# Causal mask as additions on GpSimd, and a new order of row blocks, in a fused attention, MoE and GLU kernel

## The chip, the cores and the metric

The kernel runs on one core of one Trainium2 chip. The metric is the time of one execution on the device, in microseconds (us); it is given as the median of several runs. One more execution of the same program is recorded by the profiler, and all rows below are from that one.

## What is computed

Three stages follow one another, all in fp32: causal attention with a bias made of cumulated sums (4 batches x 8 heads, 576 rows, 64 columns a head), a mixture of 8 experts in which each token goes to its best one (2304 tokens, 512 columns, 1024 hidden), and a gated unit (1536 hidden) behind an RMS norm. The change touches the attention stage.

```python
def _attn_ref(q, k, v, s):
    scores = scale * np.matmul(q, k.transpose(0, 1, 3, 2))
    causal = np.triu(np.ones((S, S), dtype=bool), k=1)
    cum = np.cumsum(np.maximum(s, 0.0), axis=-1)
    bias = -(cum[:, :, :, None] - cum[:, :, None, :])
    scores = np.where(causal, -1000000000.0, scores + np.minimum(bias, 0.0))
    attn = np.exp(scores - np.max(scores, axis=-1, keepdims=True))
    attn = attn / (np.sum(attn, axis=-1, keepdims=True) + 1e-09)
    return np.matmul(attn, v)
...
    x = _moe_ref(x=x, **moe_kwargs)      # argmax of x @ w_gate picks the expert
    return _moe2_ref(x=x, **moe2_kwargs) # (silu(xn @ w_gate) * (xn @ w_val)) @ w_out
```

## The kernel before

**Tiles.** Attention goes over 16 pairs of heads, numbered 0 to 15. The two heads of a pair lie on partitions 0 to 63 and 64 to 127, so their matmuls have 64 rows each. The 576 rows of a head make four row blocks of 128 (i = 0 to 3) and 64 last rows, those of both heads in one block (i = 4). Row block i needs the columns 0 to 128 (i + 1).

**One pair, by the names in the code.**
- `s_mm(p, i)`: for a row block two matmuls of scores (L272, one for each head, in two passes of fp32), four small bf16 matmuls that add the causal mask to the last 128 columns (L275, from the tiles `pick` and `mask`), and for each head one VectorE reduction (`reduced`, L258) that adds the cumulated sums `st.cb`, writes the scores to a tile `sc` and their extreme to `nm`. For the 64 last rows: two matmuls from `st.bd` (L285), which holds the last q columns of both heads on its diagonal blocks; GpSimd copies them there (`q_diag`, L245, two copies per pair).
- `s_exp`: ScalarE's exponential with its sum (L298), one per head and row block.
- `t_mm(p, g)`: seven groups of transposes on TensorE (L317, g = 0 to 6), each followed by ScalarE's copy into `pt` (L350).
- `pv_mm` (L363, L367): the products with v; `pv_out` (L373, L375): ScalarE's copies of the result into `vp`; `o_mm` (L391): matmuls that bring the result back into token rows and give the gate's logits; VectorE scales them (L395, L398).
- `attn_load`, `load_bias`, `load_v`: the loads of the pair after next, on the SP queue, into three input buffers (p % 3).

**What sets the order.** `attention` makes a plan: each piece of pair p has a position 10 p + POS[tag], and the pieces are issued sorted by position. With POS, the scores of pair p stand beside the transposes of pair p - 1, and the PV products of pair p - 1 follow. TensorE, VectorE, ScalarE and SP run in just that order. GpSimd's order is made by the framework's scheduler, which may put an instruction ahead of earlier ones.

**Other work in the plan.** After every four pairs (a batch), `route` ranks the tokens of the batch by expert on VectorE and then scatters their rows to `xs` in memory by five indirect DMAs on GpSimd (L485). Eight pieces of the first expert's weights are split into a high and a low part at the positions PIECES: a cast on ScalarE (L670) and a subtraction on GpSimd (L671), after which SP asks for the next raw piece. At EARLY_AT the first expert's first tokens are loaded, gated (ScalarE, L742) and transposed.

**Banks.** All PSUM tiles of attention come from one ring of eight banks, tag "b"; a tile's first matmul waits until the reader of the tile eight allocations earlier is done. The tiles `sc` form a ring of four.

Of the kernel before, what the change touches and what calls it, by code (L numbers as in the profile page):

```python
# [90 lines left out]
def masks(k):  # L91
# [3 lines left out]
    mk = slot(k, 8, [128], name="mk")  # L95
    nc.gpsimd.memset(mk, 0.0)
# [39 lines left out]
def cumulate(k):  # L136
    nc = k.nc
# [9 lines left out]
    for h in range(2):  # L147
        ps = k.psum.tile([128, 512], F32, name=f"cb{h}", tag="b")
        nc.tensor.matmul(ps[:, 0:256], k.ident[0:32, h:h + 1].broadcast_to((32, 128)), d[:, 0:256], start=True, stop=True)
        nc.scalar.copy(k.st[0].cb[:, h, 0:256], ps[:, 0:256])  # L150
# [31 lines left out]
SPLIT = ((0, 576), (576, 1152), (1152, 2176), (2176, 2752), (2752, 2880))  # L182


def attn_statics(k):
# [5 lines left out]
    def inputs(q, kk, cb, cm, bd):  # L191
        nc.gpsimd.memset(bd[0:64, 64:128], 0.0)
        nc.gpsimd.memset(bd[64:128, 0:64], 0.0)
        k.inp.append((q, kk, cb.rearrange("p (h n) -> p h n", h=2), cm, bd))
# [3 lines left out]
    inputs(first[:, 2880:3456], first[:, 3456:4032], second[:, 2880:3904], pp[0][:, 3200:3776], pp[1][:, 3200:3328])  # L198
# [27 lines left out]

def load_bias(k, p):
    st = k.st[p]
    c = 256 if p == 0 else 0
    for h in range(2):  # L230
        k.nc.sync.dma_start(out=st.cb[:, h, c:512], in_=k.cumd[2 * p + h:2 * p + h + 1, c:512].broadcast_to((128, 512 - c)))
# [11 lines left out]
def q_diag(k, p, h):  # L243
    st, r = k.st[p], slice(64 * h, 64 * h + 64)
    k.nc.gpsimd.tensor_copy(st.bd[r, r], st.q[r, 512:576])  # L245
# [16 lines left out]
def s_mm(k, p, i):  # L262
# [4 lines left out]
    if i < 4:  # L267
# [3 lines left out]
        for h, r in enumerate(rows):  # L271
            nc.tensor.matmul(ps[h], st.q[r, 128 * i:128 * i + 128], st.k[r, 0:w], start=True, stop=False)  # L272
        for n in range(2):
# [3 lines left out]
        for h in range(2):  # L277
            sc = st.s[i, h] = A.tile([128, S], F32, name=f"sc{p}_{i}_{h}", tag="sc", bufs=4)
            reduced(k, sc[:, 0:w], ps[h], st.cb[:, h, 0:w], st.nm[:, 2 * i + h:2 * i + h + 1])
# [135 lines left out]
def route(k, b):  # L415
# [66 lines left out]
    for t in range(5):  # L482
# [6 lines left out]
        of_rows(k, "placed", i.ins, k.filled)  # L489
# [142 lines left out]

# [29 lines left out]
def split(k, n=1, refill=True):  # L662
    nc = k.nc
    for _ in range(n):
        if k.staged:
# [5 lines left out]
            nc.gpsimd.tensor_tensor(w[:, :, 1, :], raw, w[:, :, 0, :].bitcast(F32), op=ALU.subtract)  # L671
# [1068 lines left out]
```

## Time and profile before

| | us |
|---|---|
| median of 3 runs | 867.74 |
| lowest and highest of them | 867.0, 867.84 |
| the profiled execution | 866.87 |
| its span, first to last instruction | 865.1 |

The profile's page gives busy time by engine: TensorE (PE) 840.1 us, VectorE (DVE) 507.6, ScalarE (ACT) 454.4, GpSimd (POOL) 365.9. Attention fills about the first 190 us. In rows of a timeline, the first number is the start in us from the span's start, the second how long the instructions of the row took together; engine, line of the kernel, operation, out<-in and shapes follow; "x4" means four instructions in a row, and a bracket tells how long the engine was idle before them and what ended that. A busy TensorE isn't one at its peak: matmul ends are modelled.

### The profile page before, as it was taken

Reading aid. Unit: us, or ns where it says so; the run is one execution under the profiler, and the core shown is the slowest. Engines: PE = TensorE matmul, PEld = TensorE weight load, DVE = VectorE, ACT = ScalarE, POOL = GpSimd, SP = SyncE. Lnnn points to the kernel's source line nnn. Section 1 sums busy time; section 2 is a strip of 40 time slices with the busy share of each in tenths; the row PEclk is TensorE's granted clock in tenths of the full one; section 3 lists DMA queues with packets and bytes.
Section 4 is the critical chain, followed back from the end, with each engine's and each line's share of the span. In section 5 each row is a group of like instructions: output and inputs, shape, how many; then the busy total and the mean of one; then the engine's idle time right before and its main releaser. Section 6 shows DMA issues by size and latency. Waiting matters only on the chain.

```text
span 865.1 us, 15488 instructions
## 1 busy us (share of the span) xinstructions
PE 840.1 (97%) x5522; PEld 750.3 (87%) x5522; DVE 507.6 (59%) x1241; ACT 454.4 (53%) x1069; POOL 365.9 (42%) x318
## 2 busy tenths in 40 slices
PE   6999999989999999999999999999999999999994
PEld 4777777779899999999999999999999988888883
DVE  5557575745415435545799988888888778400000
ACT  4988988882866565655543443333333244432310
POOL 3000431052686667677221334444444350466641
PEclk9999999999999999999999999999999999999997
DMA  6999786034575556556662332432332486521001
GB/s 208 295 325 298 251 247 201 30 118 144 197 237 191 176 175 214 185 187 194 225 191 74 128 107 104 146 112 86 103 105 102 142 325 277 204 89 38 36 37 41
DMA packets 60506, 141.45 MB, mean 164 GB/s; under 512 B 6992, under 2 KB 25451, under 8 KB 60419
## 3 DMA queue, kind: packets, MB, share of 16 engines
q1 hardware_dynamic: 57459, 130.83, 46.3%
q0 software_dynamic: 2912, 9.46, 2.9%
q8 instruction: 45, 0.74, 0.4%
q14 instruction: 42, 0.34, 0.1%
q10 hardware_dynamic: 48, 0.07, 0.0%
HBM read 105.42 MB, written 34.92 MB: 162 GB/s over the span
## 4 chain that ended last, share of the span: by engine, by line
PE 47%; DVE 3%; DMA 1%; ACT 1%; issue 1%; POOL 0%; POOLq 0%; DVEq 0%; ACTq 0%
PE gg L1166 28%; PE go L1482 17%; PE g L807 1%; DMA ringa<-ytd 1%; DVE raw L1095 0%; DVE ws L1143 0%; DVE gx1a L1410 0%; DVE raw L1098 0%; DVE h L791 0%; DVE ringa L1062 0%; DVE raw L1125 0%; DVE raw L1094 0%; DVE sq L832 0%; DVE tmp L1188 0%; DVE tmp L1186 0%
## 5 line engine op out<-in xcount | busy, mean ns | idle before, releaser
L671 POOL TENSOR_TENSOR u<-raw,u 128x1024 fp32r<-128x1024 f32 x64 | 154.8, 2429 | 73.5 <-ACT u L670 73.3
L807 PE MATMUL g<-h,u 128*128 128x256 f32 (+7 forms) x768 | 105.9, 295 | 0.7 <-DVE h L791 0.4
L787 PE MATMUL g<-xt,u 128*128 128x256 f32 (+7 forms) x768 | 104.2, 295 | 0.0
L807 PEld LDWEIGHTS g<-h,u 128*128 128x128 f32 x768 | 101.4, 188 | 1.8 <-DVE h L791 0.9
L787 PEld LDWEIGHTS g<-xt,u 128*128 128x128 f32 x768 | 101.4, 188 | 0.8
L1204 POOL TENSOR_TENSOR hs<-tmp,hs 128x384 f32<-128x384 f32 x27 | 30.3, 1123 | 106.5 <-ACT hs L1202 106.5
L258 DVE CUSTOM_DVE_ANT_0 sc<-s,in 128x128 f32<-128x128 f32 (+3 forms) x128 | 57.8, 489 | 29.2 <-ACT vp L375 16.1
L298 ACT ACTIVATE p<-sc,nm 128x128 f32<-128x128 f32 (+3 forms) x128 | 71.0, 573 | 6.8 <-DVE nm L258 6.8
L670 ACT CAST u<-raw 128x1024 fp32r<-128x1024 f32 x64 | 67.3, 1051 | 2.7 <-DMA raw<-in_w 2.7
L1166 PE MATMUL gg<-gx2a,ws 128*128 128x384 f32 x360 | 67.4, 335 | 0.6 <-DVE tmp L1188 0.6
L1166 PE MATMUL gg<-gx0a,ws 128*128 128x384 f32 x360 | 67.7, 336 | 0.0
L1166 PE MATMUL gg<-gx1a,ws 128*128 128x384 f32 x360 | 67.1, 335 | 0.0
L1487 DVE COPY raw<-go 128x256 f32<-128x256 f32 x1 | 0.4, 425 | 108.1 <-ACT raw L1486 108.1
L1166 PEld LDWEIGHTS gg<-gx2a,ws 128*128 128x128 f32 x360 | 62.8, 188 | 0.9 <-DVE tmp L1188 0.9
L1166 PEld LDWEIGHTS gg<-gx0a,ws 128*128 128x128 f32 x360 | 63.1, 188 | 0.0
L1166 PEld LDWEIGHTS gg<-gx1a,ws 128*128 128x128 f32 x360 | 62.7, 188 | 0.0
L350 ACT COPY pt<-t 128x512 f32<-128x512 f32 (+3 forms) x160 | 56.2, 449 | 10.0 <-PE t L317 8.9
L815 DVE TENSOR_TENSOR sq<-sq,sn 128x256 f32<-128x256 f32 (+6 forms) x21 | 12.7, 607 | 81.7 <-ACT sn L814 81.7
L317 PE MATMUL t<-ident,p 128*128 128x128 f32 x400 | 51.8, 275 | 0.0
L1096 ACT ACTIVATE raw<-raw 128x512 f32<-128x512 f32 x36 | 24.6, 683 | 51.7 <-DVE raw L1095 34.1
L363 PE MATMUL pvy<-pt,vp 128*64 128x512 f32 (+4 forms) x320 | 46.8, 427 | 2.9 <-ACT pt L350 2.9
L272 PE MATMUL s<-in 64*128 64x128 f32 (+3 forms) x256 | 49.5, 495 | 0.0
(307 smaller groups left out, 1704.5 us busy)
## 6 DMA issues: line engine op xcount, KB each, us to landing
raw<-in_w SPq DMA_DIRECT2D x64, 512.0 KB, 3.9
hd<-hs SPq DMA_DIRECT2D x72, 192.0 KB, 1.9
in<-cumd SPq DMA_DIRECT2D x30, 256.0 KB, 7.8
xs<-zrow SPq DMA_DIRECT2D x8, 771.0 KB, 7.1
raw<-in_wg SPq DMA_DIRECT2D x12, 512.0 KB
raw<-in_wv SPq DMA_DIRECT2D x12, 512.0 KB, 4.8
raw<-in_wo SPq DMA_DIRECT2D x12, 512.0 KB, 8.0
vp<-in_v SPq DMA_DIRECT2D x16, 320.0 KB
```

The source lines that it names most:

```text
L258: k.nc.vector.tensor_tensor_reduce(out=out, in0=ps, in1=bias, scale=-0.125, scalar=3e38, op0=ALU.add, op1=ALU.min, accum_out=accum)
L272: nc.tensor.matmul(ps[h], st.q[r, 128 * i:128 * i + 128], st.k[r, 0:w], start=True, stop=False)
L298: k.nc.scalar.activation(out, st.s[i, h][:, 0:w], AF.Exp, bias=st.nm[:, n:n + 1], scale=-1.0, accum_out=acc)
L317: nc.tensor.transpose(ps[:, off:off + 128], src[:, 128 * j:128 * j + 128], k.ident)
L350: nc.scalar.copy(b, a)
L363: nc.tensor.matmul(st.y[r, a - 64:512], st.v[:, h, j, :], k.pt[:, h, o:o + S - a], start=j == 0, stop=j == 4)
L670: nc.scalar.copy(w[:, :, 0, :], raw)
L671: nc.gpsimd.tensor_tensor(w[:, :, 1, :], raw, w[:, :, 0, :].bitcast(F32), op=ALU.subtract)
L787: nc.tensor.matmul(ps[:, 0:n], w[:, f % 4, a, 128 * kc:128 * kc + 128], x[b][:, kc, 0:n], start=kc == 0 and i == 0, stop=kc == 3 and i == 2)
L807: nc.tensor.matmul(ps[:, 0:n], w[:, f % 4, a, 128 * c:128 * c + 128], k.h[b][:, f, 0:n], start=f == 0 and i == 0, stop=f == 7 and i == 2)
L1166: k.nc.tensor.matmul(k.ps[u, bank], w[:, a, 128 * c:128 * c + 128], x[:, b, GT * c:GT * c + GT], start=first and c == 0 and n == 0, stop=c ...
L1482: k.nc.tensor.matmul(acc[g][t], c[:, a, cols], w[:, b, :], start=f == 0 and i == 0, stop=f == NF - 1 and i == 2)
```

## The change

- Pairs 1 to 15 get no mask matmuls; pair 0 keeps them. Instead GpSimd adds the mask to the cumulated sums of a head: `sums` now has six blocks of 128 per head; the four with the sums are blocks 2 to 5, and two more hold masked copies. `mask_sums(p, 0)` (one addition 128x512, one 128x256, for the first two row blocks and the last one) stands a little behind pair p - 1's first scores; `mask_sums(p, 1 + h)` (128x256 each, one per head), for row block 2, stands behind row block 1's reduction, since it writes over blocks that this reduction reads. VectorE reads the masked blocks by `bias_of`.
- The row blocks go in the order 0, 1, 3, 2, and so do their exponentials.
- `in_turn` makes GpSimd's copies of q_diag, its indirect DMAs and its weight subtractions follow the latest second `mask_sums` ahead of them in the plan.
- New positions: ROUTE, PIECES (casts now between the copies of the transposes of pairs 8 and 9), EARLY_AT (the gate behind the last pair's copies). One input buffer gets a tile of its own for the sums.

```diff
--- before.py
+++ after.py
@@ -92,8 +92,9 @@
     nc, P = k.nc, k.apool
     k.identb = P.tile([128, 128], BF16, name="identb")
     nc.vector.tensor_copy(k.identb, k.ident)
-    mk = slot(k, 8, [128], name="mk")
-    nc.gpsimd.memset(mk, 0.0)
+    k.mz = P.tile([128, 2, 128], F32, name="mz")
+    nc.gpsimd.memset(k.mz, 0.0)
+    mk = k.mz[:, 0, :]
     nc.gpsimd.affine_select(out=mk, in_=mk, compare_op=ALU.is_ge, fill=NEG, base=0,
                             pattern=[[-1, 128]], channel_multiplier=1)
     k.pick = P.tile([128, 2, 128], BF16, name="pick")
...
@@ -191,11 +192,12 @@
     def inputs(q, kk, cb, cm, bd):
         nc.gpsimd.memset(bd[0:64, 64:128], 0.0)
         nc.gpsimd.memset(bd[64:128, 0:64], 0.0)
-        k.inp.append((q, kk, cb.rearrange("p (h n) -> p h n", h=2), cm, bd))
+        k.inp.append((q, kk, cb.rearrange("p (h b n) -> p h b n", h=2, b=6), cm, bd))
 
     inputs(*(first[:, a:b] for a, b in SPLIT))
     attn_load(k, 0)
-    inputs(first[:, 2880:3456], first[:, 3456:4032], second[:, 2880:3904], pp[0][:, 3200:3776], pp[1][:, 3200:3328])
+    inputs(first[:, 3392:3968], second[:, 3392:3968], A.tile([128, 1536], F32, name="cb2"), pp[0][:, 3200:3776],
+           pp[1][:, 3200:3328])
     inputs(*(second[:, a:b] for a, b in SPLIT))
     w = slot(k, 3, [3200], name="vp")
     k.vv = [w[:, 640 * n:640 * n + 640].rearrange("p (h j d) -> p h j d", h=2, j=5) for n in range(3)]
@@ -224,11 +226,37 @@
     nc.sync.dma_start(out=st.k, in_=k.k[p])
 
 
+def sums(st, h):
+    return st.cb[:, h, 2:6, :].rearrange("p b n -> p (b n)")
+
+
+def mask_sums(k, p, n):
+    G, cb = k.nc.gpsimd, k.st[p].cb
+    sh = (128, 2, 2, 128)
+    if n == 0:
+        m = k.mz[:, 0, :].unsqueeze(1)
+        in_turn(k, G.tensor_tensor(cb[:, :, 0:2, :], cb[:, :, 3:1:-1, :], m.unsqueeze(1).broadcast_to(sh), op=ALU.add))
+        in_turn(k, G.tensor_tensor(cb[:, :, 5, :], cb[:, :, 5, :], m.broadcast_to((128, 2, 128)), op=ALU.add))
+    else:
+        h = n - 1
+        k.turn = [G.tensor_tensor(cb[:, h, 0:2, :], cb[:, h, 4:2:-1, :], k.mz, op=ALU.add).ins]
+
+
+def in_turn(k, i):
+    after(k, i.ins, k.turn)
+    return i
+
+
+def bias_of(st, i, h):
+    c = st.cb[:, h]
+    return (c[:, 1:2, :], c[:, 2::-2, :], c[:, 2::-1, :], c[:, 2:6, :])[i]
+
+
 def load_bias(k, p):
     st = k.st[p]
     c = 256 if p == 0 else 0
     for h in range(2):
-        k.nc.sync.dma_start(out=st.cb[:, h, c:512], in_=k.cumd[2 * p + h:2 * p + h + 1, c:512].broadcast_to((128, 512 - c)))
+        k.nc.sync.dma_start(out=sums(st, h)[:, c:512], in_=k.cumd[2 * p + h:2 * p + h + 1, c:512].broadcast_to((128, 512 - c)))
     for h in range(2):
         k.nc.sync.dma_start(out=st.cm[64 * h:64 * h + 64, :], in_=k.cumd[2 * p + h:2 * p + h + 1, :].broadcast_to((64, S)))
 
@@ -242,7 +270,7 @@
 
 def q_diag(k, p, h):
     st, r = k.st[p], slice(64 * h, 64 * h + 64)
-    k.nc.gpsimd.tensor_copy(st.bd[r, r], st.q[r, 512:576])
+    in_turn(k, k.nc.gpsimd.tensor_copy(st.bd[r, r], st.q[r, 512:576]))
 
 
 def copy(k, eng, out, in_):
@@ -269,14 +297,20 @@
         rows = (slice(0, 64), slice(64, 128))
         ps = [k.psum.tile([128, 512], F32, name=f"s{p}_{i}_{h}", tag="b")[:, 0:w] for h in range(2)]
         for h, r in enumerate(rows):
-            nc.tensor.matmul(ps[h], st.q[r, 128 * i:128 * i + 128], st.k[r, 0:w], start=True, stop=False)
-        for n in range(2):
+            nc.tensor.matmul(ps[h], st.q[r, 128 * i:128 * i + 128], st.k[r, 0:w], start=True, stop=p > 0)
+        for n in range(2 if p == 0 else 0):
             for h, r in enumerate(rows):
                 nc.tensor.matmul(ps[h][:, w - 128 + 64 * n:w], k.pick[r, n, :], k.mask[r, n, 64 * n:128],
                                  start=False, stop=n == 1)
         for h in range(2):
             sc = st.s[i, h] = A.tile([128, S], F32, name=f"sc{p}_{i}_{h}", tag="sc", bufs=4)
-            reduced(k, sc[:, 0:w], ps[h], st.cb[:, h, 0:w], st.nm[:, 2 * i + h:2 * i + h + 1])
+            acc = st.nm[:, 2 * i + h:2 * i + h + 1]
+            if p == 0:
+                reduced(k, sc[:, 0:w], ps[h], sums(st, h)[:, 0:w], acc)
+            else:
+                reduced(k, *(t.rearrange("p (b n) -> p b n", n=128) for t in (sc[:, 0:w], ps[h])), bias_of(st, i, h), acc)
+                if i == 1:
+                    mask_sums(k, p, 1 + h)
     else:
         sc = st.s[4, 0] = A.tile([128, S], F32, name=f"scm{p}", tag="sc", bufs=4)
         for n in range(2):
@@ -486,7 +520,7 @@
             out=k.xs, out_offset=bass.IndirectOffsetOnAxis(ap=ix[0:n, t:t + 1], axis=0),
             in_=xt[0:n, t, :], in_offset=None,
         )
-        of_rows(k, "placed", i.ins, k.filled)
+        of_rows(k, "placed", in_turn(k, i).ins, k.filled)
         k.placed.append(i.ins)
     if b == B - 2:
         V.tensor_scalar(k.na, k.base[0:1, 0:1], float(NA), None, op0=ALU.min)
@@ -566,15 +600,17 @@
     Q=[-4.0, -3.9],
     Z=[-18.4, -18.3, -7.8],
 )
-ROUTE = (34.1, 0.2)
+TURN = dict(S=(0, 1, 3, 2, 4), X=(0, 1, 2, 3, 6, 7, 4, 5, 8))
+MASK = -9.7
+ROUTE = (35.2, 0.22)
 FR = 2
-PIECES = (80.0, 81.5, 90.0, 91.5, 159.0, 161.7, 164.4, 167.1)
-EARLY_AT = (152.2, 164.0, 170.2, 170.3)
+PIECES = (81.8, 84.0, 91.8, 94.0, 159.0, 161.7, 165.3, 167.1)
+EARLY_AT = (152.2, 165.25, 170.2, 170.3)
 FILL = (12.6, 12.7, 12.8, 22.6, 22.7, 22.8, 32.5, 32.6)
 
 
 def attention(k):
-    k.st, k.todo = {}, []
+    k.st, k.todo, k.turn = {}, [], []
     with ExitStack() as es:
         k.apool = es.enter_context(k.tc.tile_pool(name="attn", bufs=1))
         cum = cumulate(k)
@@ -601,7 +637,7 @@
 
         for p in range(NP):
             for tag, fn in (("S", s_mm), ("X", s_exp), ("T", t_mm), ("V", pv_mm), ("W", pv_out), ("O", o_mm)):
-                for i, at in enumerate(POS[tag]):
+                for i, at in zip(TURN.get(tag, range(9)), POS[tag]):
                     add(10 * p + at, fn, k, p, i)
             add(10 * p + POS["N"][0], s_norm, k, p)
             for h, at in enumerate(POS["Q"]):
@@ -609,6 +645,8 @@
             for fn, at in zip((attn_load, load_bias, load_v), POS["Z"]):
                 if p > 1:
                     add(10 * p + at, fn, k, p)
+            if p:
+                add(max(10 * p + MASK, 0.6), mask_sums, k, p, 0)
             j = route(k, p // 4)
             if p == NP - 1:
                 k.last = j
...
@@ -668,7 +706,7 @@
                 new_unit(k, s, u)
             w = k.wt[s, u][:, q:q + 2]
             nc.scalar.copy(w[:, :, 0, :], raw)
-            nc.gpsimd.tensor_tensor(w[:, :, 1, :], raw, w[:, :, 0, :].bitcast(F32), op=ALU.subtract)
+            in_turn(k, nc.gpsimd.tensor_tensor(w[:, :, 1, :], raw, w[:, :, 0, :].bitcast(F32), op=ALU.subtract))
             if refill:
                 feed(k)
 
```

GpSimd's queue about pair 8, before. `in14` is the input buffer of pair 8, `in03` that of pair 9, `p16` and its copies belong to pair 10, and `xs` is where the tokens are scattered. The copies of pairs 8 and 9 are ahead of the five DMAs, and the copy that waits for the DMAs' queues (DMASW) is one for pair 10.

```order
L245 COPY in14_144<-in14_144 64x64 [waits DMAHW7_49,PE_49,Pool_49]
L245 COPY in03_143<-in03_143 64x64 [waits DMAHW6_49,PE_49,Pool_49]
L485 DMA xs_60<-xt0_539,ix0_1143 21504x514 [waits DMAHW3_49,DMAHW2_49,DMAHW4_49,DMAHW1_49,DMAHW5_49,DVE_49,Pool_49]
L485 DMA xs_60<-xt0_539,ix0_1143 21504x514 x4
L245 COPY p16_146<-in03_143 64x64 [waits DMAHW7_49,PE_49]
L245 COPY p16_146<-in03_143 64x64 [waits DMASW3_49,DMASW2_49,DMASW4_49,DMASW1_49,DMASW0_49]
L671 TENSOR_TENSOR u13_1381<-raw10_1028,u13_1381 128x2x512 [waits DMAHW5_49,Activation_49,Pool_49]
```

The same place after. `cb2` holds the sums of pair 7, `in13` is the input buffer of pair 8 with its sums, `mz` the mask. L238 and L239 are `mask_sums(8, 0)`, L273 the copies of q_diag, L242 `mask_sums(p, 1)` and `(p, 2)`.

```order
L242 TENSOR_TENSOR cb2_151<-cb2_151,mz_126 128x256 [waits DVE_49,Pool_49]
L242 TENSOR_TENSOR cb2_151<-cb2_151,mz_126 128x256 [waits DVE_49]
L238 TENSOR_TENSOR in13_144<-in13_144,mz_126 128x2x256 [waits DMAHW2_49,DMAHW1_49,Pool_49]
L239 TENSOR_TENSOR in13_144<-in13_144,mz_126 128x2x128
L519 DMA xs_60<-xt0_518,ix0_1089 21504x514 [waits DMAHW5_49,DMAHW4_49,DMAHW3_49]
L519 DMA xs_60<-xt0_518,ix0_1089 21504x514 x4
L273 COPY in13_144<-in13_144 64x64 [waits DMAHW7_49,PE_49]
L273 COPY in13_144<-in13_144 64x64 [waits DMASW2_49,DMASW3_49,DMASW1_49,DMASW4_49,DMASW0_49,Pool_49]
L242 TENSOR_TENSOR in13_144<-in13_144,mz_126 128x256 [waits DVE_49,Pool_49]
L242 TENSOR_TENSOR in13_144<-in13_144,mz_126 128x256 [waits DVE_49]
```

The copies of pair 8 are now behind the DMAs, and pair 8's two additions of row block 2 behind those copies. About pair 12 the queue is the same, with batch 1's DMAs.

ScalarE's queue at the last pair, before; `t15_g` are the transposes of pair 15, L742 is the gate, L670 the casts of weight pieces.

```order
L350 COPY pt8_160<-t15_4_2725 128x2x256
L742 ACTIVATE x0_2608<-x0_2608 128x512 x2
L670 CAST u23_2736<-raw21_2686 128x2x512
L350 COPY pt8_160<-t15_5_2739 128x2x128
L350 COPY pt8_160<-t15_5_2739 128x2x2x64
L350 COPY pt8_160<-t15_6_2746 128x2x64 x3
L670 CAST u23_2736<-raw22_2705 128x2x512
L373 COPY vp7_155<-pvx15_2760 128x64
```

The same place after:

```order
L384 COPY pt7_161<-t15_4_2546 128x2x256
L384 COPY pt7_161<-t15_5_2555 128x2x128
L384 COPY pt7_161<-t15_5_2555 128x2x2x64
L384 COPY pt7_161<-t15_6_2562 128x2x64 x3
L780 ACTIVATE x0_2429<-x0_2429 128x512 x2
L708 CAST u22_2571<-raw20_2507 128x2x512
L708 CAST u22_2571<-raw21_2526 128x2x512
L407 COPY vp6_156<-pvx15_2581 128x64
```

The gate and one cast moved from ahead of the copies of transposes 5 and 6 to behind them, and both casts now stand between the gate and the copies of the PV result.

## Rows read from the trace of the kernel before

**Rows 1.** Table by stretches: from:to, length, busy us of each engine, clock, DMA.
```profile
20.00:40.00 20.00, 20.00 (x179) 14.15 (x178) 11.82 (x57) 19.14 (x65) 0.93 (x4) 1.00 1.06 302
...
80.00:100.00 20.00, 20.00 (x181) 15.05 (x178) 12.31 (x60) 18.26 (x57) 6.43 (x10) 1.00 0.95 298
...
180.00:200.00 20.00, 17.07 (x157) 15.12 (x154) 10.60 (x42) 12.92 (x31) 10.27 (x5) 1.00 0.26 80
```

**Rows 2.** Timeline of TensorE, from pair 5's scores to pair 6's.
```profile
59.15 0.49 PE L272 MATMUL s<-in 64*128 64x128 f32 x4
59.48 0.25 PE L275 MATMUL s<-mask,pick 64*128 64x128 bf16 x4
59.56 0.68 PE L272 MATMUL s<-in 64*128 64x256 f32 x4
...
60.98 1.11 PE L272 MATMUL s<-in 64*128 64x512 f32 x4
61.92 0.25 PE L275 MATMUL s<-mask,pick 64*128 64x128 bf16 x4
62.10 1.42 PE L317 MATMUL t<-ident,p 128*128 128x128 f32 x11
...
64.61 0.93 PE L317 MATMUL t<-ident,p 128*128 128x128 f32 x7
...
67.29 1.08 PE L363 MATMUL pvy<-pt,vp 128*64 128x512 f32 x4
...
70.15 0.49 PE L272 MATMUL s<-in 64*128 64x128 f32 x4
```

**Rows 3.** Timeline of TensorE, the last pair's PV.
```profile
187.89 1.08 PE L363 MATMUL pvy<-pt,vp 128*64 128x512 f32 x4 [2.94 <-ACT pt L350]
```

**Rows 4.** Timeline of TensorE, the second pass of row block 3 in pair 5.
```profile
61.49 0.60 PE L272 MATMUL s<-in 64*128 64x512 f32 x2
```

**Rows 5.** Groups by line on GpSimd: additions of a later stage.
```profile
L1143 POOL TENSOR_TENSOR ws<-raw,ws 128x512 fp32r<-128x512 f32 x20 | 29.4, 1484 | 18.5 <-ACT ws L1138 18.5
...
L1143 POOL TENSOR_TENSOR ws<-raw,ws 128x256 fp32r<-128x256 f32 x5 | 4.1, 837 | 3.0 <-ACT ws L1138 3.0
```

**Rows 6.** Timeline of VectorE, pair 5's reductions of row blocks 1 to 3.
```profile
60.47 0.42 DVE L258 CUSTOM_DVE_ANT_0 sc<-s,in 128x256 f32<-128x256 f32 x1
...
61.28 0.56 DVE L258 CUSTOM_DVE_ANT_0 sc<-s,in 128x384 f32<-128x384 f32 x1
...
62.32 0.69 DVE L258 CUSTOM_DVE_ANT_0 sc<-s,in 128x512 f32<-128x512 f32 x1
```

**Rows 7.** Timeline of GpSimd, the scatters of batches 0 and 1.
```profile
85.95 1.15 POOL L485 DMA_INDIRECT xs<-xt,ix  x1 [0.63 <-POOL in L245]
...
91.20 0.91 POOL L485 DMA_INDIRECT xs<-xt,ix  x1 [0.30 <-issue]
...
99.12 0.23 POOL L245 COPY p<-in 64x64 f32<-64x64 f32 x1 [3.09 <-DMA xs<-xt,ix]
...
131.72 0.90 POOL L485 DMA_INDIRECT xs<-xt,ix  x1 [0.30 <-issue]
...
136.36 0.23 POOL L245 COPY in<-in 64x64 f32<-64x64 f32 x1 [2.63 <-DMA xs<-xt,ix]
```

**Rows 8.** All scatters (L485): from issue to landing.
```profile
DMA to landing us min/median/max: 2.6/3.4/8.0
```

**Rows 9.** Timeline of ScalarE, the last pair's gate, cast and copies.
```profile
184.94 1.42 ACT L742 ACTIVATE x<-x 128x512 f32<-128x512 f32 x2
186.18 1.11 ACT L670 CAST u<-raw 128x1024 fp32r<-128x1024 f32 x1
```

**Rows 10.** Timeline of TensorE, from pair 0's scores to pair 1's.
```profile
9.76 0.80 PE L272 MATMUL s<-in 64*128 64x128 f32 x4
...
13.30 2.06 PE L272 MATMUL s<-in 64*128 64x512 f32 x4
...
16.99 0.49 PE L272 MATMUL s<-in 64*128 64x128 f32 x4
```

More of the change, by code (lines that the diff above doesn't have):

```diff
@@ L149, in cumulate @@
         nc.tensor.matmul(ps[:, 0:256], k.ident[0:32, h:h + 1].broadcast_to((32, 128)), d[:, 0:256], start=True, stop=True)
-        nc.scalar.copy(k.st[0].cb[:, h, 0:256], ps[:, 0:256])
+        nc.scalar.copy(sums(k.st[0], h)[:, 0:256], ps[:, 0:256])
     load_bias(k, 0)
@@ L179 @@
 JB = (0, 576, 1024, 1344, 1536)
-SPLIT = ((0, 576), (576, 1152), (1152, 2176), (2176, 2752), (2752, 2880))
+SPLIT = ((0, 576), (576, 1152), (1152, 2688), (2688, 3264), (3264, 3392))
 def attn_statics(k):
@@ L631, in attention @@
             fn(*a)
+        k.turn = []
 RSTEPS = 40
```

## The prediction

> **What bounds the kernel now.** I read four views, from coarse to fine. First the table of busy time by 20-us stretches: from 20 to 180 us each of the eight rows (the first and the fourth are shown) has TensorE 20.00 us busy of 20.00, the next 17.07 [rows 1]. So through fourteen of the sixteen attention pairs no other engine is waited for: the matmul stream itself is the bound, and a matmul group that goes out of it is worth its issue time. Second, the timeline of one pair in the steady part (pair 5): score blocks from 59.15, the next pair's from 70.15, a period of 11.0 us [rows 2]. Third and fourth, GpSimd's (POOL) and ScalarE's (ACT) timelines at the two places where they matter: the scatters, and pair 15, whose PV waits 2.94 us for ScalarE's copies of the transposes [rows 3]. What follows attention is bound by TensorE again, so I let a change of attention's end move the whole end by as much.
>
> **The masks that go.** 15 pairs lose 16 small matmuls each. In the timeline the four masks of a row block take .08 us of issue (59.48 to 59.56; three of the four blocks are alike, the fourth, before the transposes, shows .18, part of which a change of matmul kind keeps; I count .08 for it too): 4 x .084 = .34 us. Behind the masks there is more: the first of the two 128x512 passes after them takes .51 (60.98 to 61.49), the second .43 (61.49 to 61.92) [rows 2, 4]. The blocks of 256 and 384 columns show the same .08 between first and second pass. If that excess belongs to the masks, 3 x .083 = .25 more goes. Together .59 us per pair. Pair 1 lies in the fill, where ScalarE limits, so I count 14.7 pairs: -8.7 us. If the excess belongs to something that stays, 14.7 x .34 = -5.0. I take -8.7: block 0, ahead of which there is no mask but a change of tile from PV, needs .33 for two short passes (59.15 to 59.48), about .1 more than a quarter of the .85 to .94 of two passes four times as long; so the excess shows where the kind of matmul changes, and behind masks that change goes with them.
>
> **The adds on POOL.** Each pair gets one 128x512 and three 128x256 fp32 additions. The trace has POOL additions of these shapes in a later stage: 1.48 and .84 us [rows 5]. So 4.0 us per pair on an engine that is mostly idle (busy 6.43 us of 20 from 80 to 100 us) [rows 1]. Hidden? The one chain with little room is inside the pair: VectorE's reduction of row block 1 (first head done 60.89, which is 1.74 after the pair's start, less .25 for masks of two blocks that are gone: 1.5) frees the sums of that head; the add runs to 2.34, the second head's to 3.18; VectorE takes row block 3 first, .69 and .69 us, and needs these sums only then, at about 3.0 [rows 6]. TensorE needs the PSUM bank of row block 2 back only when it starts transpose group 5 at 4.9 (64.61 - 59.15 less .59). Slack 1.3 us: nothing to pay in an ordinary pair. With row block 2 third instead of fourth the cover would be gone: its sums would be awaited at about 1.9. A VectorE pass over 128x512 takes .69, a POOL addition of that size 1.48 [rows 5, 6]. The Trainium skill ("GPSIMD Engine Reference", 3.1) has a GpSimd addition at 1.96 times VectorE's and says to use VectorE for elementwise work, which speaks against this change; by that rule the same adds on VectorE would cost some 4.0 / 1.96 = 2.0 us per pair (an estimate from that page), on an engine that is busy 12.31 of 20 us [rows 1]. The rows decide: what counts here is the engine that idles.
>
> **What the adds stand behind.** In two pairs the cover fails. q_diag's copies and the five indirect DMAs of a batch now keep POOL's program order. Before, these copies ran several pairs ahead of the DMAs, so that the copy which waits until all five scatters have landed was one for pair 10 (the copies at 99.12 and 136.36, idle 3.09 and 2.63 us) and nobody waited for it [rows 7]. Now the queue in pairs 8 and 12 reads: sums, five DMAs, the q copies of this pair, of which the second waits for all five landings, then the two adds which row block 2 of this pair needs. Behind the waiting copy stand those two adds and all of POOL; for them waits VectorE (row block 2), for its PSUM bank TensorE (transpose groups 5 and 6). Worked from pair 7's start: row block 1 reduced 1.5, two adds to 3.2, sums of pair 8 (1.48 + .84) to 5.5, five DMAs 1.31 apart (85.95 to 91.20), the last starting at 10.75. Pair 8 starts at 11.0 - .6 = 10.4. With L from the start of the last DMA to the release of the waiter, the copy starts .35 + L after pair 8's start; copy .23, add .84, reduction .56 and some .1 of signals later group 5 may start: L + 2.1 against 4.9. Group 6 waits for the second add, .4 more. The stall is L - 2.4. Before, L was 99.12 - 91.20 = 7.9 for the first batch and 136.36 - 131.72 = 4.6 for the second; all scatters of the kernel land 2.6 to 8.0 us after issue, median 3.4 [rows 7, 8]. For the first batch I take 6.3, the middle of the two, because the weight pieces that flew beside it before are now asked for later; for the second 4.6. Stalls: 3.9 and 2.2, ends of the range 0 and 5.6 for each. Batch 2's scatters come after pair 15's sums and block no add.
>
> **The last pair.** The gate (1.42 us) and one cast (1.11) stood before the copies of transposes 5 and 6 and made the 2.94 us gap [rows 3, 9]. Of these 2.5 us, which overlap by some .3, I count 2.0 as gone from the gap; some .9 stays. But now two casts come in a row ahead of the copies of the PV result, and they need raw weights whose loads are not early: I give back 1.0 (bounds 0 and 2.0). Net -1.0.
>
> **The casts of pairs 8 and 9** stand between transpose copies now, .93 us each on an engine that is busy 18.26 of 20 us there [rows 1]. One pair of them lies under the stall; +.5 for the rest (0 to 1.9).
>
> **Sum.** -8.7 - 1.0 + 3.9 + 2.2 + .5 = -3.1. The profiled execution took 866.87 us, so 863.8; it is .9 below the median of 867.74, and against the median I forecast **864.7 us**. The other loads that the change moves (the third input buffer's own tile, raw pieces behind the loads of pairs 10 and 11) change which transfer is early, and none of them was waited for: nothing.
>
> **Rivals.**
> 1. *The clock falls in the gap.* The stall of pair 8 leaves TensorE idle about 4 us in one piece. Rows: a gap of 2.94 us left the clock up (the four PV matmuls after it took 1.08, as at 67.29), while at the start, after a long stretch without matmuls, two 128x512 passes took 2.06 us against 1.11 later, until at most 16.99 [rows 2, 3, 10]. At half rate about half of a stretch is lost; 9.76 to 16.99 is 7.2 us, so up to 3.6 per fall. One fall: 864.7 + 3.5 = 868.2. The Trainium skill ("TensorE: Matmul & The Clock Gate", Part 1) says that the throttled level is the default and activity releases it; the slow start agrees (2.06 against 1.11), and no run here yet shows a gap of 4 us. 17%.
> 2. *The scatters land slowly, and the kernel is slower.* One mechanism, at the queue above: with both batches at the slowest landing of before (8.0), the stalls are 5.6 + 5.6 in place of 6.1 together: 864.7 + 5.1 = 869.8. The point from which it decides: the two L add up to 14.0 (gains of 9.2 without stalls, against L1 + L2 - 4.8); I have 10.9. For: the first batch showed 7.9. Against: the second 4.6, the median 3.4. 12%.
> 3. *No stall.* With landings at the median or below in both pairs the stalls nearly vanish (L - 2.4 is 1.0 at 3.4, and at 2.6 .2): 858.6 to 860.6. For: the median. Against: both batches' own last landings. 13%.
> 4. *The change does not do what it says:* the first-pass excess stays, since it is the cost of a new pair of PSUM banks or of weights and not of the masks: -5.0 in place of -8.7, 868.4. For: it is the same .08 in all row blocks, row block 0 too, which no mask precedes. 10%.
>
> **How the numbers follow.** Forecast 48%, rivals 17, 12, 13, 10. Eight in ten: the low end takes in most of the no-stall case (859.0), the high end the slow landings but for their extreme (869.4). About 0.2% (1.7 us) can be told from no change here: faster means below 866.0, slower above 869.5. The forecast's own spread (stalls within 1.5 us each, the tail within 1.0) puts five sixths of it below 866.0: .40; with all of rival 3 and a little of the others .58. Rivals 1 and 4 lie mostly within: same .25. Slower .17, from rival 2 and the upper parts of 1 and 4.
>
> **What would show it.** Period of ordinary pairs 10.4 in place of 11.0 (10.65 by rival 4), with second and first passes of a block alike. POOL's row for the second q copy of pairs 8 and 12 with idle time released by the scatter, followed by VectorE's row block 2 idle on POOL, and TensorE idle before transpose group 5 by some 4 and 2 us; nothing there by rival 3. The granted clock in the stretch after pair 8's gap below 1 by rival 1. The POOL additions at 1.5 and .84 us; longer ones with VectorE idle on POOL in every pair would bury the forecast. The gap before the last PV near 1 us. If the period falls by .6 and no stall shows, the time is under 861; if stalls show and the period falls by .35, it is no faster.

## The result, and the profile after

The changed kernel is slower: 873.50 us (median of 4 runs, 872.93 to 873.83) against 867.37 us before in the same session, a ratio of 1.0070 with a 95% interval of 1.0052 to 1.0087. The forecast was 864.7 with a range up to 869.4. The time lies above the range, and the sign is wrong.

The page of the profile after, its span and its busy times (us, share, instructions):

```profile
span 871.3 us, 15100 instructions
...
PE 837.5 (96%) x5282; PEld 745.4 (86%) x5282; DVE 506.0 (58%) x1241; ACT 454.4 (52%) x1069; POOL 416.1 (48%) x378
```

TensorE has 240 matmuls less and 2.6 us less busy time; GpSimd has 50.2 us more. The table by stretches, which answers to [rows 1]:

```profile
40.00:60.00 20.00, 19.62 (x151) 13.77 (x150) 9.95 (x49) 16.49 (x53) 6.03 (x10) 1.00 1.05 317
...
80.00:100.00 20.00, 16.11 (x128) 11.84 (x126) 10.73 (x51) 17.14 (x51) 10.37 (x14) 1.00 1.02 320
100.00:120.00 20.00, 19.68 (x138) 13.57 (x136) 11.33 (x52) 16.94 (x52) 15.82 (x15) 0.91 0.68 212
...
140.00:160.00 20.00, 13.34 (x88) 9.67 (x86) 7.47 (x34) 10.11 (x34) 4.47 (x9) 0.83 0.54 150
...
180.00:200.00 20.00, 18.96 (x151) 14.25 (x151) 9.94 (x43) 19.32 (x52) 12.29 (x10) 1.00 0.42 139
```

Where every row from 20 to 180 us read 20.00 before, TensorE is now idle for 3.9 us between 80 and 100 and for 6.7 between 140 and 160, and in or behind each of these stretches the clock column is below 1. The waits of TensorE and the timeline give the two places (idle time before the row, and what ended it, in the bracket):

```profile
46.73 2.43 PE L300 MATMUL s<-in,in 64*128 64x128 f32 x16
49.09 1.42 PE L351 MATMUL t<-ident,p 128*128 128x128 f32 x11
...
51.61 0.93 PE L351 MATMUL t<-ident,p 128*128 128x128 f32 x7
...
54.29 1.08 PE L397 MATMUL pvy<-pt,vp 128*64 128x512 f32 x4
...
57.14 2.43 PE L300 MATMUL s<-in 64*128 64x128 f32 x16
...
99.74 1.58 PE L351 MATMUL t<-ident,p 128*128 128x128 f32 x7 [3.90 <-DVE nm L286]
...
104.37 1.08 PE L397 MATMUL pvy<-pt,vp 128*64 128x512 f32 x4
...
151.06 1.76 PE L351 MATMUL t<-ident,p 128*128 128x128 f32 x7 [6.66 <-DVE nm L286]
...
155.72 1.08 PE L397 MATMUL pvy<-pt,vp 128*64 128x512 f32 x4
```

The first five rows are an ordinary pair: scores from 46.73, the next pair's from 57.14, 10.41 us in place of 11.0 [rows 2]. The other rows are pairs 8 and 12: their transpose group 5 (it starts 4.9 us after the scores in an ordinary pair) waits for VectorE. VectorE itself waits for GpSimd, and GpSimd for the scatters:

```profile
90.94 0.90 POOL L519 DMA_INDIRECT xs<-xt,ix  x1 [0.30 <-issue]
91.84 0.25 POOL L273 COPY in<-in 64x64 f32<-64x64 f32 x1
98.05 0.23 POOL L273 COPY in<-in 64x64 f32<-64x64 f32 x1 [5.96 <-DMA xs<-xt,ix]
98.37 1.40 POOL L242 TENSOR_TENSOR in<-in,mz 128x256 f32<-128x256 f32 x2
...
139.32 0.90 POOL L519 DMA_INDIRECT xs<-xt,ix  x1 [0.30 <-issue]
140.22 0.25 POOL L273 COPY in<-in 64x64 f32<-64x64 f32 x1
149.37 0.23 POOL L273 COPY in<-in 64x64 f32<-64x64 f32 x1 [8.90 <-DMA xs<-xt,ix]
149.69 1.40 POOL L242 TENSOR_TENSOR in<-in,mz 128x256 f32<-128x256 f32 x2
```
```profile
150.44 0.56 DVE L286 CUSTOM_DVE_ANT_1 sc<-s,in 128x384 f32<-128x384 f32 x1 [7.81 <-POOL in L242]
```

These are the rows that answer to [rows 7]: the same wait of the second q copy for the landings, but now two mask additions (L242) and row block 2 stand behind it. The landing came 98.05 - 90.94 = 7.1 us after the last scatter's start in the first batch and 149.37 - 139.32 = 10.05 in the second. TensorE's clock behind the gaps, from the table by stretches (the third figure from the end; 0.50 is the lower of its two levels, 1.2 of 2.4 GHz, and 0.57 a stretch mostly at it):

```profile
100.00:104.00 4.00, 3.97 (x17) 3.06 (x15) 2.18 (x10) 3.23 (x12) 3.86 (x5) 0.57 0.21 79
...
150.00:154.00 4.00, 2.94 (x12) 2.85 (x13) 2.48 (x10) 1.73 (x6) 3.45 (x6) 0.50 0.26 76
```

From group 5 to the PV products it is 2.68 us in the ordinary pair (51.61 to 54.29), 4.63 in pair 8 and 4.66 in pair 12.

Counted from score block to score block, pairs 8 and 12 take 16.4 and 19.2 us, 6.0 and 8.8 more than their like. In this execution pairs 5 and 6 take .8 and 1.1 more. The loads of the sums land late there, and the additions stand between landing and reduction: the first reductions, at 59.60 and 70.82, start as the addition ends that waited for the load (58.30 to 59.56 and 69.53 to 70.79). Three later executions on one chip (q_ahead, q_on_vector, dummy_transposes) show at most .4 more in the two together; seven on two other chips show .8 to 2.1. Pair 9, with two of the casts, takes .4 more. Pairs 6, 10 and 14 hold the ranking of a batch's tokens, and it costs them .5 us each where it cost .2: with the new ROUTE its small matmuls (rk) stand in the middle of the PV products, where they stood ahead of them. The place in pair 10:

```profile
128.03 0.19 PE L490 MATMUL rk<-oh,tri 128*128 128x40 bf16 x1
...
128.36 0.66 PE L397 MATMUL pvy<-pt,vp 128*64 128x192 f32 x8
```

Pair 15's PV waits .77 us where it waited 2.94 [rows 3], and from pair 15's scores to the first expert product it is 21.8 us instead of 23.8. In sum the first expert product starts at 201.77 instead of 193.53, 8.2 us later. TensorE's end is 8.05 us later, the span only 6.2 longer: the last scatter of the output lands 1.8 us faster after its issue. The code there is the same, and nothing here says why.

### The profile page after: what moved, and what is told of

It reads as the page before. It is cut to its first block, busy times and chain, and to the rows that moved or that the text cites. A ratio compares the mean times of both kernels' runs of the same rounds, so it can differ in the third digit from the quotient of the medians.

```text
span 871.3 us, 15100 instructions
## 1 busy us (share of the span) xinstructions
PE 837.5 (96%) x5282; PEld 745.4 (86%) x5282; DVE 506.0 (58%) x1241; ACT 454.4 (52%) x1069; POOL 416.1 (48%) x378
## 4 chain that ended last, share of the span: by engine, by line
PE 46%; DVE 3%; DMA 1%; ACT 1%; issue 1%; POOL 0%; POOLq 0%; DVEq 0%; ACTq 0%
PE gg L1204 28%; PE go L1520 17%; PE g L845 1%; DMA ringa<-ytd 1%; DVE raw L1133 0%; DVE ws L1181 0%; DVE gx1a L1448 0%; DVE raw L1136 0%; DVE h L829 0%; DVE ringa L1100 0%; DVE raw L1163 0%; DVE raw L1132 0%; DVE sq L870 0%; DVE tmp L1226 0%; DVE tmp L1224 0%
## 5 line engine op out<-in xcount | busy, mean ns | idle before, releaser
L351 PE MATMUL t<-ident,p 128*128 128x128 f32 x400 | 54.0, 280 | 11.5 <-DVE nm L286 11.3
L351 PEld LDWEIGHTS t<-ident,p 128*128 128x128 f32 x400 | 45.1, 142 | 21.3 <-DVE nm L286 20.9
L829 DVE SCALAR_TENSOR_TENSOR h<-g,h 128x256 fp32r<-128x256 f32 (+7 forms) x64 | 26.7, 446 | 29.8 <-ACT h L828 29.8
```

The costliest lines, as they stand in the source:

```text
L351: nc.tensor.transpose(ps[:, off:off + 128], src[:, 128 * j:128 * j + 128], k.ident)
L829: nc.vector.scalar_tensor_tensor(hl[:, f, 0:n], ps[:, 0:n], 0.0, hh[:, f, 0:n].bitcast(F32), op0=ALU.max, op1=ALU.subtract)
```

## The experiments

The kernel before was run beside each. On the chip of the first four it took 867.57 us, on two others 876.2 and 876.7: from loads_14_later on, ratios count, not microseconds. The changed kernel itself was not run on these two.

**q_on_vector**: the q copies on VectorE.

```diff
-    in_turn(k, k.nc.gpsimd.tensor_copy(st.bd[r, r], st.q[r, 512:576]))
+    k.nc.vector.tensor_copy(st.bd[r, r], st.q[r, 512:576])
...
-    Q=[-4.0, -3.9],
+    Q=[1.05, 1.06],
```

> The changed kernel, with q_diag's copies on VectorE (behind the reductions of the same pair) instead of GpSimd; nothing is left out. Theory (the queue): the loss is the second q copy, which waits on GpSimd for the scatters to land with two mask additions behind it; with the copies gone from GpSimd no instruction there waits for a landing. In the changed kernel pair 8 took 6.0 us and pair 12 8.8 us more than an ordinary pair's 10.4; both excesses go: 873.5 - 14.8 = 858.7, in a range of 857 to 862, TensorE without a gap over 1 us from pair 2 to pair 14, granted clock 1.00 throughout. Rival (the scatters' traffic or the additions themselves hold pairs 8 and 12 up): the gaps stay, 868 or more.

Measured: 872.74 us, ratio 1.0048 (1.0029 to 1.0068). A miss in time, by a cause that neither side had. The waits before transpose group 5 are gone, and no instruction on GpSimd waits for the scatters' landing in pairs 8 and 12. But pairs 8 and 9 now wait elsewhere. TensorE, VectorE and GpSimd at that place:

```profile
102.16 2.26 PE L319 MATMUL sm<-in 128*128 128x288 f32 x4 [3.66 <-DVE in L273]
```
```profile
97.54 4.48 DVE L273 COPY in<-in 64x64 f32<-64x64 f32 x2
```
```profile
97.31 4.66 POOL L709 TENSOR_TENSOR u<-raw,u 128x1024 fp32r<-128x1024 f32 x2
```

Two copies of 64x64 took 4.48 us: they ended just when GpSimd's two subtractions did. It happened in pair 9 too (3.66 us again), and the clock column behind both gaps reads 0.50. From `sm` to the next pair's scores it is 7.37 us in pair 8 (102.16 to 109.53) and 7.24 in pair 9, where an ordinary pair takes 4.27 (52.87 to 57.14): here a fall of the clock cost about 3 us.

**q_ahead**: the change as it is, with one pair of numbers moved, so that the copies stand ahead of the five scatters in GpSimd's queue.

```diff
-    Q=[-4.0, -3.9],
+    Q=[-9.65, -9.64],
```

> The changed kernel, with only the positions of q_diag's copies moved from -4.0 and -3.9 to -9.65 and -9.64, so that GpSimd makes them ahead of the five scatters of a batch. The copies that wait for the landings are then those of pairs 9 and 13, one pair later, behind the additions of pairs 8 and 12. Theory (the queue): the wait stays on GpSimd, as long as before, but nobody needs what is behind it before pair 9's or 13's row block 2, 13.4 us after the start of pair 8 or 12: no gap over 1 us in pairs 8 and 12, 858.7 to 862. Rival (additions or traffic): as before, 868 or more. If landings take over 11 us, a rest of the stall shows in pair 9 or 13.

Measured: 858.46 us, ratio 0.9888 (0.9863 to 0.9913). The queue theory gave 858.7 to 862. GpSimd in pair 8 of this kernel:

```profile
90.29 0.91 POOL L519 DMA_INDIRECT xs<-xt,ix  x1 [0.30 <-issue]
91.26 1.42 POOL L242 TENSOR_TENSOR in<-in,mz 128x256 f32<-128x256 f32 x2
92.77 1.28 POOL L238 TENSOR_TENSOR in<-in,mz 128x512 f32<-128x512 f32 x1
94.00 0.74 POOL L239 TENSOR_TENSOR in<-in,mz 128x256 f32<-128x256 f32 x1
94.67 0.24 POOL L273 COPY in<-in 64x64 f32<-64x64 f32 x1
97.42 0.23 POOL L273 COPY in<-in 64x64 f32<-64x64 f32 x1 [2.51 <-DMA xs<-xt,ix]
```

The landing is as slow as ever (7.1 us from 90.29), the wait is still there, but the additions of pair 8 are through at 92.7, and those of pair 9 start at 102.40. TensorE has no gap above .3 us between pair 2 and pair 14, and pairs 8 and 12 take 10.78 and 10.41 us. The additions, the scatters and their traffic are all still in this kernel; so the loss is the place of the copies in the queue.

**dummy_transposes**: more work in front of the gaps.

```diff
     elif g == 4:
-        for h in range(2):
-            for i in range(2, 4):
-                tr(256 * h + 128 * (i - 2), ph[i][h], 2)
+        for _ in range(9 if p in (7, 11) else 1):
+            for h in range(2):
+                for i in range(2, 4):
+                    tr(256 * h + 128 * (i - 2), ph[i][h], 2)
```

> The changed kernel with more work: in pairs 7 and 11, transpose group 4 is done nine times over (32 more fp32 transposes, 3.5 us), right ahead of the gap in which TensorE waits in pairs 8 and 12. Theory of the clock: the matmuls behind the two gaps ran at the lower granted clock (0.57 and 0.50 in the stretches behind them), which cost 1.6 to 2.0 us each; with gaps of .4 and 3.1 us left the clock stays up, and the kernel gets 3 to 4 us faster by doing more: about 870. Rival (the slow stretch behind the gap is due to late PSUM banks or copies and not to the clock): no faster than 873, and where the dummies outlast the wait, slower.

Measured: 869.87 us (867.62 to 872.39 in 10 runs), ratio to the kernel before 1.0015 (0.9997 to 1.0034), where the changed kernel had 1.0070: 3.6 us less with 7 us of work more. That difference isn't the price of the clock alone, since the landings differed too (7.85 and 7.68 us after the last scatter's start, where they were 7.1 and 10.05), and with them the waits. Both stretches behind the gaps show the full clock:

```profile
99.00:103.00 4.00, 3.60 (x22) 2.61 (x24) 3.16 (x15) 2.88 (x10) 3.78 (x6) 1.00 0.31 107
...
146.00:150.00 4.00, 3.32 (x20) 2.46 (x22) 3.16 (x13) 2.90 (x11) 3.04 (x6) 1.00 0.26 76
```

Group 5 to PV takes 2.98 in both pairs (99.38 to 102.36, 146.66 to 149.64). So of the 1.95 us that pair 8 lost there, .30 is the second addition's delay and 1.65 the clock; in pair 12 it is .30 and 1.68. So the size rests on the trace.

**tail_alone**: the kernel before with the last pair's gate and cast moved.

```diff
-PIECES = (80.0, 81.5, 90.0, 91.5, 159.0, 161.7, 164.4, 167.1)
-EARLY_AT = (152.2, 164.0, 170.2, 170.3)
+PIECES = (80.0, 81.5, 90.0, 91.5, 159.0, 161.7, 165.3, 167.1)
+EARLY_AT = (152.2, 165.25, 170.2, 170.3)
```

> The kernel before with only the two positions at the last pair changed: the gate at 165.25 instead of 164.0 and one cast at 165.3 instead of 164.4, so that both stand behind the last pair's copies. The prediction's term for this was -1.0 (bounds -2.0 and 0). The trace of the changed kernel shows .77 + .57 + .34 us of TensorE gaps there instead of 2.94: -1.3. If the gap behind it is refilled by the raw weight's load, 0.

Measured: 864.86 us, ratio 0.9981 (0.9963 to 0.9999): by the ratio 1.7 us less, with an interval from .1 to 3.2, by the medians 2.7. The gap is as in the changed kernel, and behind it only one of .33 us is new:

```profile
185.26 1.08 PE L363 MATMUL pvy<-pt,vp 128*64 128x512 f32 x4 [0.77 <-ACT pt L350]
...
194.35 0.19 PE L456 MATMUL rk<-oh,tri 128*128 128x40 bf16 x1 [0.33 <-DVE oh L450]
```

**loads_14_later**: the changed kernel, with pair 14's loads of q, k and sums after batch 1's scatters.

```diff
-                    add(10 * p + at, fn, k, p)
+                    add(10 * p + at + (6.0 if p == 14 and fn is not load_v else 0.0), fn, k, p)
```

> The changed kernel with the loads of q, k and sums of pair 14 asked for six positions later, so that they no longer fly beside batch 1's scatters. Theory (the landing is mis-sized because of traffic): in the changed kernel these loads went out at 136.3 to 138.7 us and the scatters at 134.2 to 139.3, and the last landing was seen 10.1 us after the last scatter's start, against 4.6 before; with the loads out of the way the landing falls below 5 us, pair 12 takes 13 us or less in place of 19.2, and its gap is too short for the clock to fall: 867 to 869.5. Rival (the scatters are slow of themselves on this queue): landing 7 or more, pair 12 at 17 or more, 872 to 874.

Measured: ratio 0.9898 (0.9851 to 0.9944), 868.66 us on a chip where the kernel before takes 876.16. The forecast of 867 to 869.5 was for the first chip. Neither this time nor this ratio can be set beside the changed kernel's, which didn't run here; the trace can. GpSimd at batch 1 of this kernel:

```profile
140.53 0.90 POOL L519 DMA_INDIRECT xs<-xt,ix  x1 [0.30 <-issue]
141.44 0.24 POOL L273 COPY in<-in 64x64 f32<-64x64 f32 x1
143.35 0.23 POOL L273 COPY in<-in 64x64 f32<-64x64 f32 x1 [1.67 <-issue]
```

The copy runs 2.8 us after the last scatter's start, in place of 10.05; pair 12 takes 11.5 us in place of 19.2, with no gap above .21 us, and the clock stays up. Pair 8, whose loads were left, still has its gap of 3.93 us and a clock of 0.57 behind it; its landing took 7.2 us (92.13 to 99.37), as in the changed kernel, so it isn't the chip that lands faster. So the second landing was slow because of what flew beside it.

**rows_in_order**: q_ahead, with row blocks 0, 1, 2, 3.

```diff
-TURN = dict(S=(0, 1, 3, 2, 4), X=(0, 1, 2, 3, 6, 7, 4, 5, 8))
+TURN = dict()
```

> The kernel of q_ahead (q copies ahead of the scatters) with the row blocks in the old order 0, 1, 2, 3. The prediction said that with row block 2 third the cover of the additions is gone: the sums are ready about 2.4 and 3.2 us after the pair's start plus signals, VectorE wants them at about 1.9. If so, VectorE ends some .7 us later in each pair and TensorE waits for PSUM banks by .2 to .5 in each of 14 pairs: 861 to 865. Rival (slack of 1.3 us on TensorE's side is enough in either order): 858.5, the same as q_ahead.

Measured: ratio 0.9877 (0.9834 to 0.9920), beside 0.9888 and 0.9871 for q_ahead. VectorE's reductions of row block 2, and TensorE's pairs:

```profile
49.48 0.56 DVE L286 CUSTOM_DVE_ANT_1 sc<-s,cb 128x384 f32<-128x384 f32 x1 [0.56 <-POOL cb L242]
```
```profile
47.06 2.43 PE L300 MATMUL s<-in,in 64*128 64x128 f32 x16
...
57.47 2.00 PE L300 MATMUL s<-in 64*128 64x128 f32 x14
```

VectorE does wait for GpSimd, .56 us, as was said; TensorE doesn't in such an ordinary pair: it takes 10.41 us in either order. In pair 5, where the sums land late, TensorE did wait for VectorE, .74 and .36 us, and the pair took 12.25 us, against 11.21 in the changed kernel. So the new order bought nothing in ordinary pairs, perhaps something in a late one, and nothing that the times of these runs can see.

**casts_spread** and **casts_spread_tail**: q_ahead with the weight pieces elsewhere.

```diff
-PIECES = (81.8, 84.0, 91.8, 94.0, 159.0, 161.7, 165.3, 167.1)
+PIECES = (81.8, 91.8, 101.8, 111.8, 159.0, 161.7, 165.3, 167.1)
...
+PIECES = (81.8, 91.8, 101.8, 111.8, 159.0, 165.3, 170.6, 170.7)
```

> The kernel of q_ahead with the first four weight pieces one per pair (81.8, 91.8, 101.8, 111.8) in place of two in pair 8 and two in pair 9. In q_ahead's trace the three pairs from 8 on take .37, .84 and .2 us more than their like, with TensorE waiting .3 us for copies of the transposes in two of them: the prediction's term for the casts was .5. If ScalarE's two casts in one pair are the cause, 1.0 to 1.4 goes: 857.2. If not, 858.5.

> As casts_spread, and at the last pair the sixth piece stands behind the copies of the transposes (165.3) and the last two behind the first tokens' transposes (170.6, 170.7). The .78 us gap ahead of the last PV and part of the .61 behind it belong to casts between the copies: another -1.0, 856.2. Rival (the pieces are then too late for the first expert's second product, 12 us later): no gain, or a gap there.

Measured: ratios 0.9843 (0.9803 to 0.9883) and 0.9864 (0.9822 to 0.9906). Pair 9, 11.25 us in q_ahead, takes 10.41 (103.87 to 114.28), so the casts' part of the theory holds in that pair. Pair 10 takes 11.64 in place of 11.17, with a wait of .69 us of the ranking's matmuls for VectorE: the two pairs together gain .4, where 1.0 to 1.4 was expected of pairs 8 to 10. In the second kernel the gap ahead of the last PV falls from 2.22 us to 1.27, and more is lost behind the start of the experts, where the ranking's matmuls wait 2.35 us, in place of .36 in the first.

```profile
185.16 1.08 PE L397 MATMUL pvy<-pt,vp 128*64 128x512 f32 x4 [1.27 <-ACT pt L384]
196.23 0.19 PE L490 MATMUL rk<-oh,tri 128*128 128x40 bf16 x1 [2.35 <-DVE oh L484]
```

**q_ahead_again** and **casts_spread_again**, on one chip:

> q_ahead once more, on the same chip as the next, since the kernel before took 867.6 us on one chip and 876.2 on another. Theory: a ratio of .986 to .991 to the kernel before on either chip.

> casts_spread once more beside q_ahead on one chip. In its first trace the pairs behind the casts took 10.41 us each (9 to 10 and 10 to 11 less the ranking) where q_ahead had 11.25 and 11.17, so the theory of the casts gives 1.0 us less than q_ahead; the rival, no difference.

Measured: 865.36 us, ratio 0.9871 (0.9825 to 0.9918), and 865.10, ratio 0.9860 (0.9818 to 0.9902). No difference. From pair 8's to pair 15's scores casts_spread took 78.5 us against 79.7; from there to the first expert product 24.4 against 22.7. Of the 1.2 gained only .2 is in pairs 9 and 10; .9 is in pair 8. On this chip pairs 8 and 12 of q_ahead still took 13.4 and 12.3 us, with rows of TensorE that start in the middle of the scores after gaps of .7 and 1.0. For the first gap the trace names nothing, for the second ScalarE's copy `vp`, which itself waited for TensorE's scores; VectorE's first reductions came 2.6 and 2.9 us after the start of the scores, where it is .66 in an ordinary pair. All seven runs on the two slower chips lose some 1 to 4 us in each of these pairs beside any stall by the queue; what holds the scores up there stays open.

**q_on_vector_early**: q_on_vector, with the copies behind row block 0.

```diff
-    Q=[1.05, 1.06],
+    Q=[0.115, 0.116],
```

> The kernel of q_on_vector with the copies at another place in VectorE's order: behind row block 0's reductions (0.115, 0.116) instead of behind the whole pair's (1.05, 1.06). In q_on_vector the two copies of 64x64 together took 4.48 us in pairs 8 and 9, from 97.54 to 102.02, while GpSimd's two weight subtractions ran from 97.31 to 101.97; TensorE waited 3.66 us for them, twice, and the clock fell behind it. Theory (a VectorE copy and a GpSimd addition exclude one another for the whole instruction): at the new place GpSimd does no subtraction, the copies take .2 to .4 us, both gaps go: 858 to 861 on a chip on which the kernel before takes 867.5 (a ratio of about .990). Rival (these copies are slow on VectorE in themselves, or the third and last cause is the scatter traffic): gaps as in q_on_vector, ratio 1.00 or more.

Measured: ratio 0.9858 (0.9814 to 0.9902) against 1.0048 for q_on_vector. The groups by line, first of this kernel, then of q_on_vector (mean ns of one copy behind the comma):

```profile
L273 DVE COPY in<-in 64x64 f32<-64x64 f32 x22 | 4.3, 195 | 0.2
```
```profile
L273 DVE COPY in<-in 64x64 f32<-64x64 f32 x22 | 12.3, 558 | 0.1
```

The same copies, 195 ns in place of 558, and both gaps ahead of `sm` are gone. The copies aren't slow; beside a GpSimd subtraction they have to wait for its end. It is a second way to the same gain, without any wait for the landings. Pair 8 still took 14.4 us there, by the open loss of this chip.

## Why the prediction was wrong, step by step

| step | forecast | measured | by |
|---|---|---|---|
| masks | -.59 per pair | -.59 per pair | 11.0 to 10.41 |
| last pair | -1.0 | -1.7 alone (-.1 to -3.2) | tail_alone |
| pair 8, stall | 3.9 (L 6.3) | 4.2 (3.90 + .30; L 7.1) | trace |
| pair 12, stall | 2.2 (L 4.6) | 7.0 (6.66 + .30; L 10.05) | trace |
| clock behind the gaps | 0 | 1.65 + 1.68 | dummy_transposes |
| casts | +.5 | +.4, in pair 9 | trace |
| ranking's new place | no term | +.3 in each of three pairs | trace |
| late sums, pairs 5 and 6 | 0 | +1.9 in the profiled execution, at most .4 in three others, .8 to 2.1 on two other chips | trace |

- *What bounds the kernel*, *the masks that go*: right, and to a few hundredths. The first pass of a row block is no longer slower than the second (47.49 to 47.92 and 47.92 to 48.35 for the two passes of 512 columns; each row below begins with one pass and runs on into the next): the excess went with the masks, and rival 4 falls.

```profile
47.49 1.03 PE L300 MATMUL s<-in,in 64*128 64x512 f32 x4
47.92 1.24 PE L300 MATMUL s<-in,in 64*128 64x512 f32 x6
48.35 0.81 PE L300 MATMUL s<-in,in 64*128 64x384 f32 x4
```

- *What the adds stand behind*: the mechanism, the pairs, the engines that wait and the formula (stall = L - 2.4, with L of 7.1 giving 4.7 against 4.2 measured, and 10.05 giving 7.65 against 6.96) were right, the formula with up to .7 us too much. q_ahead shows it by moving two numbers. **The term that was mis-sized is L of the second batch**: I took 4.6 from the row of before and 8.0 as the end of the range, from the slowest scatter there [rows 7, 8]. In that kernel the second batch's scatters started 1.0 us after pair 11's scores; now they start 5.3 us after them, as my own chain said (5.5), and so beside the loads of the pair after next (SP's queue, changed kernel):

```profile
136.25 0.33 SPq L226 DMA_DIRECT2D in<-in_k  x1
136.67 0.89 SPq L259 DMA_DIRECT2D in<-cumd  x2
137.65 1.10 SPq L261 DMA_DIRECT2D in<-cumd  x2
139.47 0.34 SPq L266 DMA_DIRECT2D vp<-in_v  x1
```

  These four rows of SP's queue lie within the scatters of 134.2 to 140.2. loads_14_later moved the loads and L fell to 2.8. I had carried over a landing without asking what would fly beside it at its new time. The L of the first batch, 6.3 for 7.1, came near with a wrong reason: the weight pieces are asked for later, as I said, but at 91.35 and 92.55, so they still fly beside the landing (90.94 to 98.05).
- **The step that failed worst is how the cases were put together.** The fall of the clock stood as a rival to the stall, at 17%, with one fall. It is a consequence of the stall: my own forecast had TensorE idle for 3.9 us in pair 8, and the only row that spoke for a clock that stays up was one of 2.94. Both gaps were longer than that, and the clock was low behind both. The price, 3.5 a fall from the first matmuls of the kernel [rows 10], was too high for these two falls (1.65 and 1.68) and near that of the two in q_on_vector (about 3). Rivals 1 and 2 came true together: 864.7 + (17.2 - 10.9) + 3.3 = 874.3, against 873.5 measured. That it comes so near is luck in part: the sum leaves out the late sums (1.9) and the ranking (.9) on one side, the excess of the formula (1.2) and the faster landing of the output (1.8) on the other. Rival 2 had the right break-even, L1 + L2 = 14.0; they were 17.2. The range, up to 869.4, held rival 1 (868.2), ended just below rival 2 (869.8), and had no room for both.
- *The adds on POOL*: hidden in an ordinary pair, as said. They took 1.28 and .73 us in place of 1.48 and .84. That the cover is gone with row block 2 third was wrong: VectorE waits .56 us (rows_in_order), which the slack of 1.3 us on TensorE's side covers in an ordinary pair. The figure for that slack stood in the same paragraph, and I didn't hold the claim against it.
- *The pages that the prediction drew on*: the clock read 0.57 and 0.50 of full speed behind 3.9 and 6.7 us without a matmul, and 1.00 behind 1.9 and .8 us in dummy_transposes. The Trainium skill ("TensorE: Matmul & The Clock Gate", Part 1) says that the throttled state is the default and activity releases it; these traces agree. With the additions on GpSimd and its queue in order, q_ahead is 1.1% faster than the kernel with the masks on TensorE. The Trainium skill ("GPSIMD Engine Reference", 3.1) has the rule to leave elementwise work to VectorE; no run here has these additions on VectorE, so which of the two engines is the better place stays untested.

## What to carry to other kernels

Before work is given to an idle engine, list what else its queue holds and which entry waits for something slow; the price of the move is what then stands behind that entry, and a change of two numbers of order was worth 15 us here. A transfer's time holds only with the traffic that it was measured in: when a stage gets shorter or a start moves, look up what the queue of loads will do at that moment. And a stall on TensorE is costed with the slow matmuls that follow it, in the same case and not in another.

## What the runs showed of the hardware

- A VectorE copy of 64x64 between two places in SBUF waits for a GpSimd two-input instruction to end: 4.48 us for two copies beside 4.66 us of GpSimd, against 195 ns for one without. The Trainium skill ("SBUF — State Buffer", Who interferes with whom) states this lock: VectorE copies can take both pairs of ports, one of which is GpSimd's, and who comes second waits for the whole instruction. The traces agree. VectorE's `tensor_scalar` on 128x10 shows it too: in the changed kernel .17 us at 51.21, with GpSimd idle, and .52 at 151.94, until an addition ended.
- The reductions from PSUM, beside the same additions, kept their time: .69 us at 48.69 and at 49.31 in the changed kernel, with additions from 48.39 to 49.81, as in [rows 6].
- A gap of 2.94 us left TensorE's clock up, one of 3.66 (q_on_vector) or 3.90 did not; a fall cost 1.65 and 1.68 us in the changed kernel and about 3 in q_on_vector. In dummy_transposes, where transposes left gaps of 1.90 and .79 us, it read 1.00. The gap that the trace shows isn't the whole story: in pair 8 of q_on_vector_early one of 1.42 us had 0.53 behind it (96 to 98 us), and that pair's scores are the ones that were held up for an open reason.
- Scatters of 1.18 MB landed 2.8 us after the last one's start with pair 14's loads held back, and 10.05 us (7.68 in dummy_transposes) with k and the sums of that pair, 1.1 MB, beside them.
